# Two attention + GLU layers on one core: output normalization partly on GpSimd, layer norms in pairs, and a new order

## The chip, the cores and the metric

The kernel runs on one core of a Trainium2 chip. The time is device time in microseconds of one launch; several runs of a kernel are made and their median is given. The core's engines that matter here are TensorE (PE, with its weight loads PEld), VectorE (DVE), ScalarE (ACT), GpSimd (POOL) and SyncE (SP), whose queue carries nearly all DMAs.

## The reference

The input is x, 2048 rows (tokens) of 512 numbers in bf16. Two blocks are applied, and then the same two again with the same weights:

```python
def _layernorm(x, axis=-1, eps=1e-5):
    m = jnp.mean(x, axis=axis, keepdims=True)
    v = jnp.var(x, axis=axis, keepdims=True)
    return (x - m) / jnp.sqrt(v + eps)

def _A_ref(x, wqkv, wo):            # 32 heads of 16, window of 256 keys, causal
    q, k, v = split_heads(x @ wqkv)
    scores = einsum("bhqd,bhkd->bhqk", q, k) * (16 ** -0.5)
    scores = where(mask, scores, -1e9)      # 0 <= query - key < 256
    o = einsum("bhqk,bhkd->bhqd", softmax(scores), v)
    return merge_heads(o) @ wo

def _B_ref(x, w_gate, w_up, w_down):        # hidden width 1792
    return (sigmoid(x @ w_gate) * (x @ w_up)) @ w_down

x = x + _A_ref(_layernorm(x), A_wqkv, A_wo)
x = x + _B_ref(_layernorm(x), B_w_gate, B_w_up, B_w_down)
x = x + _A_ref(_layernorm(x), A_wqkv, A_wo)
x = x + _B_ref(_layernorm(x), B_w_gate, B_w_up, B_w_down)
```

`split_heads` and `merge_heads` stand here for the reference's reshapes and transposes.

## The kernel before

x stays in SBUF (`xsb`) as 16 tiles of 128 tokens. All the weights are loaded once.

For each tile and layer the work is this.

- **Layer norm** (`layer_norm`). VectorE computes the statistics (L600, L602). GpSimd adds the epsilon (L612) and raises to the power -1/2 (L613); this step is called `root`. VectorE applies them (L629) into a buffer `xn`. TensorE transposes the tile in four blocks (L647), and ScalarE or VectorE copies the result out of PSUM into `xnT` (L676 or L678, the lines of the copy helper). The normed tile feeds Q, K and V (key `"p"`) or the GLU (key `"g"`).
- **Q, K, V** (L713, L744, L780). The first two are computed for groups of four tiles, 512 columns at a time, apart from a few units of the first group that are cut by tile. K is split into even and odd heads by two multiplications on VectorE (L759).
- **Attention scores** in visits: a visit fills four PSUM banks (`Sps`) with scores (L1039, L1050, L1060), and ScalarE takes their exponential in one instruction (L1092) into `PTring` or `edge`. VectorE multiplies the borders of the window by masks (L970).
- **Values** (L1119): 80 small matmuls for half of the heads of a tile. The V matrix has a column of ones for each head, so the sum of the exponentials comes out beside the output. Two copies bring both halves into `OTs` (L676 or L678).
- **Normalization of the output** (`after_values`). VectorE turns the tile in 32 x 32 blocks (L1138, `OTs` to `Oq`), takes the reciprocals of the sums (L1144, `Rt`), multiplies in two instructions, one for even and one for odd heads (L1146, `On`), and turns the result back (L1151, `OnT`). Then TensorE applies the output projection (L903), VectorE adds it to x (L909), and the layer norm of the GLU begins.
- **GLU** (L808): gate and up projections, ScalarE's tanh (L826, the sigmoid in another form) and VectorE's product (L834) into `hT`, in groups of one, two or four tiles that `GLU` lists. Then the down projection (L872) and its sum with x (L881), followed by the next layer's norm or the output's DMA.

The order of all instructions is fixed when the program is built. The class `Plan` acts the engines' time out with a duration for each task, and whenever an engine falls free in it, the ready task with the lowest number in `PRIO` (later `LATE_PRIO`) goes next; TensorE's next work is chosen by `pick` and `choose`, with `RANK`. `PACE` holds the least time between visits in the plan: its entries 2 and 3 hold before the visit given by entry 4, after that entry 0 is for the first layer and entry 1 for the second. On the chip, each engine runs its instructions in the order that came out, and waits by semaphores. The duration and the priority stand in the call that makes a task:

```python
b = pl.task({"DVE": 1130}, turn, [box[0], box[1]], self.prio["oq0" if early else "oq"], lambda: self.has("Oq"), port=True)
c = pl.task({"DVE": 1030}, norm, [b.done], self.prio["no0" if early else "no"], lambda: self.has("On"), port=True)
d = pl.task({"DVE": 600}, turn2, [c.done], self.prio["on0" if early else "on"], lambda: self.has("OnT"), port=True)
```

`port=True` makes the plan keep such a task from running beside another task so marked on VectorE or GpSimd. Buffers come in rings (`ring`); there is one `OTs`, one `Oq`, one `Rt`, one `On` and two `OnT`.

Of the kernel before, what the change touches and what calls it, by code (L numbers as in the profile page):

```python
# [9 lines left out]
ALU = mybir.AluOpType  # L10
# [46 lines left out]
def pool_ns(n):  # L57
# [5 lines left out]
GLU = [[[1, 1, 1, 1, 2, 2], [1, 1, 1, 1, 2, 2], [1, 1, 2, 2, 2], [1, 1, 1, 1, 1, 1, 1, 1], [2, 2, 2, 2], [1, 1, 1, 1, 1, 1, 1, 1], [2, 2, 4]], [[4, 4, 4, 4], [4, 4, 4, 2, 1, 1], [4, 4, 2, 1, 1, 4]]]  # L63
PACE = [2681.81, 1328.37, 1196.7, 872.42, 21.95]
EARLY = 16
# [17 lines left out]
PRIO = dict(st_x0=8.026, ap_x0=7.059, xt_x0=10.785, st_x1=3.545, ap_x1=6.693, xt_x1=8.977, st_x=12.044,  # L83
    ap_x=12.327, xt_x=-6.634, st_p=-1.733, ap_p=4.349, xt_p=1.138, st_g=-6.356, ap_g=3.74, xt_g=-5.594,
    st_g0=3.292, ap_g0=-10.915, xt_g0=-4.847, tp=7.272, tp_g=6.212, q=-0.67, q0=11.129, q1=-22.989,
    k=-9.747, k0=14.768, k1=0.61, s=-5.3, s0=4.016, s1=2.634, v=0.444, v0=23.378, v1=20.074, vv=-6.331,
    exp=-13.785, exp0=-0.049, m0=3.46, m00=4.795, e0=-8.802, e00=0.423, e1=-0.562, e10=9.011, m2=-6.041,
    m20=0.716, th=15.676, mu=-10.778, dn=-20.12, add=2.096, add0=7.831, out=-15.994, mv=31.961, mv0=5.964,
    oq=-8.579, oq0=-11.733, no=13.392, no0=-3.279, on=11.451, on0=-10.714, vc=11.541, vc0=-1.273)
OPT = dict(gu='SP', g1=0, bk=3, bq=3, wide=0, r0=2, g0=5, g2=0, x0=1, eps=1, hold=1, own=1, ck=0, cq=2,  # L90
    turn=2, split=0, mo=0, at=3, r1=3, near=3)
SLACK = dict(xt=5595, oq=812, on=1665, vc=730)
RANK = dict(tp=-16.462, o=-6.977, lead=17.162, far=65.44, v=20.015, g=58.528, d=32.436, feed=40.797,
    x3=34839.477, wd=1492.629, go=176.096)
LATE_PRIO = dict(st_p=-4.956, ap_p=38.034, xt_p=0.962, st_x=-1.619, ap_x=-5.199, xt_x=17.448, st_g=-14.573,
    ap_g=-6.614, xt_g=0.299, q=-17.247, k=34.931, s=-1.549, v=-6.237, exp=-43.312, m0=4.641, e0=8.453,
    e1=11.689, m2=17.496, th=2.747, mu=-20.998, dn=2.523, add=-6.022, out=27.029, mv=45.566, oq=-5.883,
    no=8.561, on=11.817, vc=-20.116)
LATE_SLACK = dict(xt=541, oq=5451, on=4000, vc=10531)
LATE_RANK = dict(tp=52.672, o=-17.659, lead=2.057, far=12.106, v=-5.627, g=-3.049, d=10.813, feed=-60.763,  # L100
    go=344.346)
# [271 lines left out]
class Net:  # L373


    def __init__(self, ctx, tc, A_x, wqkv, wo, w_gate, w_up, w_down, out):
# [44 lines left out]
        ring("xn", 4, [P, 1, D])  # L421
# [164 lines left out]
    def layer_norm(self, key, t, deps):  # L586

        nc, pl = self.nc, self.pl
        done = self.xn_ready[key, t]
        box = {}  # L590
# [5 lines left out]
        def stats(e):  # L596
            if "st" not in box:
                box["st"] = self.take("st")
            st = box["st"][0][:, 0]
            nc.vector.bn_stats(out=st[:, 0:6], in_=self.xsb[:, t, :])  # L600
            if not first:
                nc.vector.bn_aggr(out=st[:, 6:8], in_=st[:, 0:6])  # L602

        def moments(e):
            st = box["st"][0][:, 0]
            nc.vector.bn_aggr(out=st[:, 6:8], in_=st[:, 0:6])
            nc.vector.tensor_scalar(out=st[:, 9:10], in0=st[:, 7:8], scalar1=1e-5, scalar2=None, op0=ALU.add)

        def root(e):
            st = box["st"][0]  # L610
            if not first:
                nc.gpsimd.tensor_scalar(out=st[:, 0, 9:10], in0=st[:, 0, 7:8], scalar1=1e-5, scalar2=None, op0=ALU.add)  # L612
            nc.gpsimd.tensor_tensor(out=st[:, 0, 8:9], in0=st[:, 0, 9:10], in1=self.nhalf[:, 0:1], op=ALU.pow)  # L613
# [10 lines left out]
        def apply(e):  # L624
            box["xn"] = b = self.take("xn")
            if key not in self.xnT:
                self.xnT[key] = self.take("xnT")
            st = box["st"][0][:, 0]
            nc.vector.tensor_scalar(out=b[0][:, 0, :], in0=self.xsb[:, t, :], scalar1=st[:, 6:7], scalar2=st[:, 8:9],  # L629
                                    op0=ALU.subtract, op1=ALU.mult)  # L630
# [6 lines left out]
        b = pl.task({"POOL": 800 - 230 * first}, root, [a.done], self.prio["st_" + kind])  # L637
        self.roots[key + (t,)] = b.done
        c = pl.task({"DVE": 406}, apply, [b.done], self.prio["ap_" + kind], can, port=True)
# [3 lines left out]
        i = t % NBG  # L643
        def steps(bank):
            pt = self.tp_view(bank)
            xn = box["xn"][0][:, 0]
            return [(57, lambda c=c: nc.tensor.transpose(pt[:, c, :], xn[:, c * P:(c + 1) * P], self.ident[:]))  # L647
                    for c in range(KT)]

        def evac(u):  # L650
            pt = self.tp_view(u.bank)
            if key == ("p", 0, 0) and t < OPT["split"]:
                half, both = KT // 2, Event()
                when_all([pl.task({e: ns}, lambda e, o=o: self.copy(e, self.xnT[key][0][:, i][:, o:o + half], pt[:, o:o + half]), [u.done],
                                  self.prio["tp"] - 9).done for e, ns, o in (("ACT", act_ns(half * P), 0), ("DVE", dve_ns(half * P) + 50, half))], both.fire)
                both.then(lambda: (self.give(box["xn"]), done.fire()))
                return both
            d = pl.task({"ACT": act_ns(KT * P), "DVE": dve_ns(KT * P) + 100}, lambda e: self.copy(
                e, self.xnT[key][0][:, i], pt), [u.done], self.prio["tp" if key[0] == "p" else "tp_g"])
            d.done.then(lambda: (self.give(box["xn"]), done.fire()))  # L660
            return d.done

        def ready():
            u = Unit(("tp", t), steps, [], False, evac)
            if key == ("p", 0, 0) and OPT["own"]:
                u.own = BANKS + t
            self.streams[0].append(u)

        c.done.then(ready)
# [455 lines left out]
    def after_values(self, L, t, half, bank, done):  # L1125
# [13 lines left out]

        def norm(e):  # L1140
            box["Rt"], box["On"] = self.take("Rt"), self.take("On")
            Oq, Rt, On = box["Oq"][0], box["Rt"][0], box["On"][0]
            tv = Oq[:].rearrange("p c (b r) -> p c b r", r=32)
            nc.vector.reciprocal(out=Rt[:], in_=tv[:, :, :, 16:17])  # L1144
            for e in range(2):
                nc.vector.tensor_tensor(out=On[:, :, :, e, :], in0=tv[:, e:8:2, :, 0:16],  # L1146
                                        in1=Rt[:, e:8:2].to_broadcast([P, 4, 4, 16]), op=ALU.mult)
# [10 lines left out]
        b = pl.task({"DVE": 1130}, turn, [box[0], box[1]], self.prio["oq0" if early else "oq"], lambda: self.has("Oq"), port=True)  # L1158
        b.done.then(lambda: self.give(box["OTs"]))
        c = pl.task({"DVE": 1030}, norm, [b.done], self.prio["no0" if early else "no"], lambda: self.has("On"), port=True)  # L1160
        c.done.then(lambda: (self.give(box["Oq"]), self.give(box["Rt"])))
        d = pl.task({"DVE": 600}, turn2, [c.done], self.prio["on0" if early else "on"], lambda: self.has("OnT"), port=True)
# [324 lines left out]
```

## Time and profile before

| | |
|---|---|
| median of 3 runs | 565.57 us (565.51 to 566.4) |
| the profiled execution | 566.81 us |
| its span, first to last instruction | 565.1 us |
| PE busy | 548.7 us (97%) |
| VectorE busy | 461.9 us (82%) |
| ScalarE busy | 407.8 us (72%) |
| GpSimd busy | 61.4 us (11%) |
| granted TensorE clock | 1.0 |

The profile gives every instruction's start and end with its line in the kernel. A row of a group reads: line, engine, operation, what it writes and reads, shape, count, then busy time in us and the mean ns of one, then the engine's idle time before these instructions and what ended most of it. A row of waits reads: engine, tile and line that waited, what it waited for, total us, times, and the longest. The first layer's attention runs to about 260 us, the second layer's from about 285 to 490 us in bursts; after about 496 us only GLU work of the second layer is left. DMA is busy mostly in the first 60 us.

### The profile page before, as it was taken

What the parts mean: (1) busy time and instruction counts of PE and PEld (TensorE: products, weight loads), DVE (VectorE), ACT (ScalarE), POOL (GpSimd) and SP (SyncE); (2) the same over time, 40 slices, a digit from 0 to 9 for tenths busy, and PEclk for the clock granted to TensorE, in tenths of its full rate; (3) what the DMA queues carried; (4) which work ended last, traced back from release to release, by engine and by line L of the source; (5) the groups of instructions that cost most, each with busy time, mean ns of one, the idle gap of its engine ahead of it and who ended that gap; (6) DMA issues with size and microseconds to landing.
All of it is one profiled execution on the core that took longest, in us unless ns stands there. A gap on an engine that the chain in (4) does not pass through costs nothing.

```text
span 565.1 us, 22076 instructions
## 1 busy us (share of the span) xinstructions
PE 548.7 (97%) x9998; PEld 300.0 (53%) x9998; DVE 461.9 (82%) x921; ACT 407.8 (72%) x424; POOL 61.4 (11%) x153
## 2 busy tenths in 40 slices
PE   8999899999999999999999999999999999999997
PEld 7446565854788645444444444544444444544443
DVE  6999999999988899996699986989768999852332
ACT  3999989979999887891699827999189985530330
POOL 4411111111101120101100011000100001000000
PEclk9999999999999999999999999999999999999999
DMA  8723000000000000000000000000100000000001
GB/s 254 294 92 106 3 24 2 23 3 23 4 23 3 23 3 23 23 2 1 11 2 23 3 13 11 2 23 3 40 20 2 23 3 31 12 1 20 19 0 38
DMA packets 18574, 17.38 MB, mean 31 GB/s; under 512 B 1841, under 2 KB 17457, under 8 KB 18481
## 3 DMA queue, kind: packets, MB, share of 16 engines
q1 hardware_dynamic: 17360, 14.93, 8.1%
q8 instruction: 78, 1.28, 0.9%
q10 hardware_dynamic: 1120, 1.05, 0.6%
q14 instruction: 16, 0.12, 0.1%
HBM read 9.70 MB, written 2.10 MB: 21 GB/s over the span
## 4 chain that ended last, share of the span: by engine, by line
PE 66%; DVE 21%; ACT 5%; issue 4%; DMA 2%; ACTq 1%; POOL 0%; SPq 0%; DVEq 0%
PE bank L808 29%; PE bank L872 14%; PE bank L1119 6%; PE Sps L1039 5%; PE bank L903 5%; DVE PTring L970 3%; DVE kTp L759 3%; PE bank L713 2%; DVE Oq L1138 2%; PE bank L780 2%; DVE edge L970 2%; ACT PTring L1092 2%; DVE On L1146 2%; DVE st L600 1%; DMA wg<-in_B_w_gate_dram 1%
## 5 line engine op out<-in xcount | busy, mean ns | idle before, releaser
L1092 ACT ACTIVATE PTring<-Sps 128x2048 bf16<-128x2048 f32 (+1 forms) x122 | 226.7, 1859 | 29.2 <-PE Sps L1039 26.6
L808 PE MATMUL bank<-xnT,wg 128*128 128x128 bf16 (+1 forms) x784 | 125.7, 288 | 1.3 <-ACT xnT L676 0.9
L808 PE MATMUL bank<-xnT,wu 128*128 128x128 bf16 (+1 forms) x784 | 125.6, 288 | 0.0
L872 PE MATMUL bank<-wd,hT 128*128 128x512 bf16 (+2 forms) x462 | 103.3, 373 | 0.0
L834 DVE SCALAR_TENSOR_TENSOR hT<-hT,bank 128x512 bf16<-128x512 bf16 (+1 forms) x140 | 78.0, 570 | 27.0 <-PE bank L808 23.1
L826 ACT ACTIVATE hT<-bank 128x512 bf16<-128x512 f32 (+1 forms) x140 | 69.3, 518 | 33.3 <-PE bank L808 33.1
L808 PEld LDWEIGHTS <-wg 128*128 128x128 bf16 x784 | 58.9, 98 | 40.4 <-issue 4.0
L808 PEld LDWEIGHTS <-wu 128*128 128x128 bf16 x784 | 59.1, 98 | 38.3 <-issue 2.3
L872 PEld LDWEIGHTS <-hT 128*128 128x128 bf16 x462 | 42.9, 98 | 49.2 <-issue 1.6
L612 POOL TENSOR_SCALAR st<-st 128x1 f32<-128x1 f32 x60 | 17.8, 297 | 426.1 <-DVE st L602 426.0
L1092 ACT ACTIVATE edge<-Sps 128x2048 bf16<-128x2048 f32 (+1 forms) x32 | 56.9, 1777 | 8.8 <-PE Sps L1050 8.1
L676 ACT COPY xnT<-bank 128x512 bf16<-128x512 bf16 x36 | 20.1, 603 | 46.4 <-PE bank L647 46.4
L1119 PE MATMUL bank<-PTring,Vaug 128*32 128x64 bf16 (+1 forms) x2880 | 52.5, 203 | 0.7 <-DVE PTring L970 0.5
L1039 PE MATMUL Sps<-qT,kTp 32*128 32x256 bf16 (+3 forms) x1216 | 47.5, 248 | 3.7 <-ACT PTring L1092 1.9
L1119 PEld LDWEIGHTS <-Vaug 128*32 128x32 bf16 x2880 | 44.1, 97 | 13.1 <-issue 11.1
L600 DVE BATCH_NORM_STATS2 st<-xsb 128x6 f32<-128x512 bf16 x64 | 43.7, 683 | 2.6 <-DMA xsb<-in_A_x_dram 2.2
L1119 PE MATMUL bank<-edge,Vl 128*32 128x64 bf16 x1024 | 44.2, 193 | 0.9 <-DVE edge L970 0.7
L881 DVE SCALAR_TENSOR_TENSOR xsb<-bank,xsb 128x512 bf16<-128x512 f32 (+2 forms) x33 | 22.0, 665 | 28.1 <-PE bank L872 28.0
L970 DVE TENSOR_TENSOR PTring<-PTring,mask 128x1024 bf16<-128x1024 bf16 x64 | 43.3, 678 | 1.2 <-ACT PTring L1092 1.0
L1039 PEld LDWEIGHTS <-kTp 32*128 32x128 bf16 x1216 | 18.8, 92 | 44.1 <-issue 41.1
L1138 DVE STREAM_TRANSPOSE Oq<-OTs 128x1024 bf16<-128x1024 bf16 x32 | 39.7, 1240 | 1.6 <-ACT OTs L676 1.0
L1119 PE MATMUL bank<-edge,Vh 128*32 128x64 bf16 x896 | 40.8, 193 | 0.0
(70 smaller groups left out, 691.0 us busy)
## 6 DMA issues: line engine op xcount, KB each, us to landing
Vl<-Vaug SPq DMA_DIRECT2D x32, 68.0 KB, 2.2
out_dram<-xsb SPq DMA_DIRECT2D x15, 128.0 KB, 2.1
Vh<-Vaug SPq DMA_DIRECT2D x28, 68.0 KB, 2.2
wg<-in_B_w_gate_dram SPq DMA_DIRECT2D x2, 896.0 KB, 9.2
wu<-in_B_w_up_dram SPq DMA_DIRECT2D x2, 896.0 KB, 11.8
wd<-in_B_w_down_dram SPq DMA_DIRECT2D x7, 256.0 KB, 3.7
xsb<-in_A_x_dram SPq DMA_DIRECT2D x6, 256.0 KB, 5.7
wq<-in_A_wqkv_dram SPq DMA_DIRECT2D x3, 256.0 KB, 5.7
```

The lines of the kernel that those rows point to most:

```text
L600: nc.vector.bn_stats(out=st[:, 0:6], in_=self.xsb[:, t, :])
L808: return [(mm_ns(w), lambda i=i, j=j, fc=fc, wt=wt, kt=kt: self.nc.tensor.matmul(pt[:, i, j, :], lhsT=wt[:, kt, fc * P:(fc + 1) * P], rhs= ...
L826: self.nc.scalar.activation(out=self.hT[:, ch[0] * GW:ch[0] * GW + size], in_=pt, func=AF.Tanh, scale=0.5)
L834: self.nc.vector.scalar_tensor_tensor(out=h, in0=h, scalar=1.0, in1=pt, op0=ALU.add, op1=ALU.mult)
L872: nc.tensor.matmul(self.banks[bank][:, 0:w], lhsT=self.hT[:, at:at + P], rhs=self.wd[:, fc, d], start=fc == 0, stop=fc == FC - 1)
L881: e = pl.task({"DVE": dve_ns(w)}, lambda e: nc.vector.scalar_tensor_tensor(out=self.xsb[:, t, d], in0=self.banks[u.bank][:, 0:w], scalar=0 ...
L903: return [(mm_ns(D), lambda c=c: nc.tensor.matmul(self.banks[bank][:], lhsT=b[0][:, c, :], rhs=self.wot[:, c, :], start=c == 0, stop=c == ...
L970: done = pl.task({"DVE": dve_bf_ns(1024)}, lambda e: nc.vector.tensor_tensor(out=r, in0=r, in1=m.to_broadcast([P, 16, HP]), op=ALU.mult), ...
L1039: nc.tensor.matmul(self.sps[:, m, o:o + n * HP], lhsT=kTp[32 * m:32 * m + 32, i, tt, e, :], rhs=self.qT[32 * m:32 * m + 32, i, q0:q0 + n * ...
L1092: nc.scalar.activation(out=out, in_=src, func=AF.Exp, scale=scale)
L1119: nc.tensor.matmul(o, lhsT=Va[:, c0:c0 + 32], rhs=p(h), start=k == 0 or t == 0, stop=k == len(parts) - 1 or t == 0, tile_position=(0, 32 * g))
L1138: nc.vector.transpose(out=box["Oq"][0][:].rearrange("p c q -> p (c q)"), in_=box["OTs"][0][:].rearrange("p c q -> p (c q)"))
```

## The change

In `after_values` the reciprocal becomes a task of its own on VectorE, and the two multiplications become a task on GpSimd, between the first and the second turn. This task has no `port` mark.

In `layer_norm` two neighbouring tiles share one task for the root, one task for applying (two instructions), one unit of eight transposes and one copy out of PSUM, which is 1024 wide. The first group of four tiles and the first two tiles of the first GLU stay alone, as all were. The `xn` ring has two buffers of two tiles in place of four of one.

The durations given to the plan change (1130 to 1260, 600 to 725, and others), and with them all its priorities, ranks and paces. The choice of the first layer's GLU groups changes: `g0` selects eight groups of one tile before, and 1, 1, 2, 2, 2 after, each followed by 4, 4. The second layer's (`g2`) are four of four in both. Of the first K and Q units, two and one are cut by tile, where it was three and three.

```diff
-GLU = [[[1, 1, 1, 1, 2, 2], [1, 1, 1, 1, 2, 2], [1, 1, 2, 2, 2], [1, 1, 1, 1, 1, 1, 1, 1], [2, 2, 2, 2], [1, 1, 1, 1, 1, 1, 1, 1], [2, 2, 4]], [[4, 4, 4, 4], [4, 4, 4, 2, 1, 1], [4, 4, 2, 1, 1, 4]]]
-PACE = [2681.81, 1328.37, 1196.7, 872.42, 21.95]
-EARLY = 16
+GLU = [[[1, 1, 2, 2, 2], [1, 1, 1, 1, 2, 2], [1, 1, 2, 2, 2], [1, 1, 1, 1, 2, 2], [2, 2, 2, 2], [1, 1, 1, 1, 1, 1, 1, 1], [2, 2, 4]], [[4, 4, 2, 1, 1, 1, 1, 2], [4, 2, 2, 4, 1, 1, 2], [4, 4, 4, 4]]]
+PACE = [1944.11, 1222.78, 405.97, 655.26, 5.98]
+EARLY = 12
...
-OPT = dict(gu='SP', g1=0, bk=3, bq=3, wide=0, r0=2, g0=5, g2=0, x0=1, eps=1, hold=1, own=1, ck=0, cq=2,
-    turn=2, split=0, mo=0, at=3, r1=3, near=3)
+OPT = dict(gu='SP', g1=0, bk=2, bq=1, wide=0, r0=2, g0=2, g2=2, x0=1, eps=1, hold=1, own=1, ck=0, cq=2,
+    turn=2, split=0, mo=0, at=3, r1=1, near=3)
...
-        ring("xn", 4, [P, 1, D])
+        ring("xn", 2, [P, 2, D])
...
+        alone = key[:2] == ("p", 0) and t < NBG * (1 + OPT["g1"]) or key[0] == "g" and key[1] * NT + t < 2
...
-        box = {}
+        if alone:
+            box, tiles = {"i": 0}, [t]
+        else:
+            box = self.pairs.setdefault((key, t // 2), {"i": t % 2, "ready": []})
+            tiles = [t // 2 * 2, t // 2 * 2 + 1]
...
+            for k, tt in enumerate(tiles):
+                st = box["st"][0][:, k]
+                nc.vector.tensor_scalar(out=b[0][:, k, :], in0=self.xsb[:, tt, :], scalar1=st[:, 6:7], scalar2=st[:, 8:9],
+                                        op0=ALU.subtract, op1=ALU.mult)
...
+        if not alone:
+            box["ready"].append(a.done)
+            if len(box["ready"]) < 2:
+                return
+        b = pl.task({"POOL": 800 - 230 * first}, root, box.get("ready", [a.done]), self.prio["st_" + kind])
...
+            def steps(bank):
+                pt = self.tp_view(bank, 2 * KT)
+                xn = box["xn"][0][:].rearrange("p t d -> p (t d)")
+                return [(57, lambda c=c: nc.tensor.transpose(pt[:, c, :], xn[:, c * P:(c + 1) * P], self.ident[:]))
+                        for c in range(2 * KT)]
+
+            def evac(u):
+                d = pl.task({"ACT": act_ns(2 * KT * P), "DVE": 670}, lambda e: self.copy(
+                    e, self.xnT[key][0][:, i:i + 2].rearrange("p t c q -> p (t c) q"), self.tp_view(u.bank, 2 * KT)),
+                    [u.done], self.prio["tp" if key[0] == "p" else "tp_g"])
...
+        def invert(e):
+            box["Rt"] = self.take("Rt")
+            nc.vector.reciprocal(out=box["Rt"][0][:], in_=box["Oq"][0][:].rearrange("p c (b r) -> p c b r", r=32)[:, :, :, 16:17])
+
         def norm(e):
-            box["Rt"], box["On"] = self.take("Rt"), self.take("On")
+            box["On"] = self.take("On")
...
-            nc.vector.reciprocal(out=Rt[:], in_=tv[:, :, :, 16:17])
             for e in range(2):
-                nc.vector.tensor_tensor(out=On[:, :, :, e, :], in0=tv[:, e:8:2, :, 0:16],
+                nc.gpsimd.tensor_tensor(out=On[:, :, :, e, :], in0=tv[:, e:8:2, :, 0:16],
                                         in1=Rt[:, e:8:2].to_broadcast([P, 4, 4, 16]), op=ALU.mult)
...
-        b = pl.task({"DVE": 1130}, turn, [box[0], box[1]], self.prio["oq0" if early else "oq"], lambda: self.has("Oq"), port=True)
+        b = pl.task({"DVE": 1260}, turn, [box[0], box[1]], self.prio["oq0" if early else "oq"], lambda: self.has("Oq"), port=True)
...
-        c = pl.task({"DVE": 1030}, norm, [b.done], self.prio["no0" if early else "no"], lambda: self.has("On"), port=True)
+        i = pl.task({"DVE": 370}, invert, [b.done], self.prio["no0" if early else "no"], lambda: self.has("Rt"), port=True)
+        c = pl.task({"POOL": 1300}, norm, [i.done], self.prio["no0" if early else "no"], lambda: self.has("On"))
...
-        d = pl.task({"DVE": 600}, turn2, [c.done], self.prio["on0" if early else "on"], lambda: self.has("OnT"), port=True)
+        d = pl.task({"DVE": 725}, turn2, [c.done], self.prio["on0" if early else "on"], lambda: self.has("OnT"), port=True)
```

`PRIO`, `SLACK`, `RANK`, `LATE_PRIO`, `LATE_SLACK` and `LATE_RANK` get new numbers throughout.

## The prediction

> **What bounds the kernel now.** I read the page's busy times first, then the same times in stretches of 20 us, then the waits, then single rows for prices.
>
> ```profile
> PE 548.7 (97%) x9998; PEld 300.0 (53%) x9998; DVE 461.9 (82%) x921; ACT 407.8 (72%) x424; POOL 61.4 (11%) x153
> ...
> PE 66%; DVE 21%; ACT 5%; issue 4%; DMA 2%; ACTq 1%; POOL 0%; SPq 0%; DVEq 0%
> ```
>
> TensorE is busy for 548.7 of 565.1 us, so its idle time is 16.4 us. VectorE holds a fifth of the chain that ended last, GpSimd none of it.
>
> ```profile
> 40.00:60.00 20.00, 17.93 (x448) 12.61 (x451) 19.76 (x44) 18.97 (x23) 4.26 (x10) 1.00 0.23 75
> ...
> 120.00:140.00 20.00, 20.00 (x397) 9.35 (x396) 19.59 (x40) 17.16 (x15) 3.06 (x6) 1.00 0.06 18
> 140.00:160.00 20.00, 19.20 (x559) 14.51 (x558) 17.04 (x36) 18.04 (x20) 2.10 (x4) 1.00 0.04 10
> ...
> 500.00:520.00 20.00, 20.00 (x95) 9.00 (x94) 6.92 (x11) 4.19 (x7) 0.00 (x0) 1.00 0.03 11
> ```
>
> In the stretches of 20 us the columns are PE, PEld, DVE, ACT, POOL. From 20 to 260 us (twelve rows, three of them above) DVE adds up to 226.2 of 240 us, or 94%, and PE to 233.0: first-layer attention runs on three full engines, and 7.0 us of PE's idle time lie there. From 280 to 500 us DVE is at 189.9 of 220 us and PE idles 2.1 us. After 500 us PE is alone. Less VectorE work can therefore pay mostly before 260 us.
>
> ```profile
> PE Sps L1039 <- ACT PTring L1092: 1.9, 4, 0.8
> ...
> PE bank L647 <- DVE Vaug L678: 1.2, 4, 0.6
> ...
> PE Sps L647 <- DVE xn L629: 1.1, 1, 1.1
> ...
> PE bank L808 <- ACT xnT L676: 0.9, 1, 0.9
> ...
> PE bank L1119 <- DVE edge L970: 0.7, 3, 0.4
> ```
>
> These are PE's own waits (total, times, longest). Those for VectorE (the three here, PTring 0.5, xnT 0.5, xn 0.3) make 4.3 us. A busy PE hides more: taking the ends of matmul records one after another and subtracting columns times 0.42 ns (the chain's 112 matmuls of 512 columns take 24.33 us) and about 0.12 to 0.16 us for each change between the three kinds of matmul (dense, scores, values), I count 29.7 us in 200 places above 60 ns each. About 11 us of it end on VectorE, 9 on ScalarE, the rest on nothing visible. So 4.3 to 11 us is all that a perfect VectorE could give back.
>
> **Prices** come from the groups of instructions by shape (busy time, then mean ns of one) and from three places of the timeline (start and length in us).
>
> ```profile
> L613 POOL TENSOR_TENSOR st<-st,nhalf 128x1 f32<-128x1 f32 x64 | 38.5, 602 | 11.1 <-DVE st L607 6.1
> ...
> L1146 DVE TENSOR_TENSOR On<-Oq,Rt 128x256 bf16<-128x256 bf16 x64 | 24.4, 422 | 1.1
> L676 ACT COPY xnT<-bank 128x512 bf16<-128x512 bf16 x36 | 20.1, 603 | 46.4 <-PE bank L647 46.4
> ...
> L678 DVE COPY xnT<-bank 128x512 bf16<-128x512 bf16 x24 | 9.3, 415 | 0.4 <-PE bank L647 0.3
> ...
> L1092 ACT ACTIVATE edge<-Sps 128x1024 bf16<-128x1024 f32 x4 | 4.1, 1033 | 2.0 <-PE Sps L1050 1.9
> ```
> ```profile
> 192.85 0.66 DVE L970 TENSOR_TENSOR PTring<-PTring,mask 128x1024 bf16<-128x1024 bf16 x1
> 193.03 0.57 POOL L612 TENSOR_SCALAR st<-st 128x1 f32<-128x1 f32 x1 [12.33 <-DVE st L602]
> ```
> ```profile
> 493.47 0.22 POOL L612 TENSOR_SCALAR st<-st 128x1 f32<-128x1 f32 x1 [13.91 <-DVE st L602]
> ```
> ```profile
> 12.79 0.68 DVE L759 TENSOR_SCALAR kTp<-kTp,rm 128x512 bf16<-128x512 bf16 x1 [0.35 <-ACT kTp L676]
> 12.80 0.47 POOL L543 MEMSET Vaug<- 128x64 bf16 x1
> ```
>
> **Multiplications to GpSimd.** VectorE loses 64 instructions, 24.4 us (0.76 a tile); 16 tiles, 12.2 us, belong to the full first layer. GpSimd gains 64. No row shows such an instruction there. Lower bound: VectorE's 0.42 us. Upper: 0.94, the longest L613. I take 0.65, half of the 1300 ns which the new code itself reckons for both, in the middle of the rows; that is 41.6 us in all. The pair's path grows by 1.3 - 0.76 = 0.5 us a tile, plus one more hop. Cover: from the end of the first turn (L1138) to the start of the second (L1151) the trace has 1.7 to 6.3 us, 3.8 on the mean of 32 tiles (117.3 to 122.0 for one), much of it other VectorE work, and PE has dense GLU work meanwhile. I cost it at 0; if the cover is gone it is 32 times 0.5, 16 us. Behind the multiplications on GpSimd's queue stand the roots (L612, L613) of a norm, which then wait up to 1.3 us, and apply (L629) behind them.
>
> **Who waits when both engines run.** A GpSimd instruction of 0.22 us took 0.57 when it met a mask multiplication (L970), and ended when that did; 12 of 60 L612 did so. The other way, L759 took 0.68 us instead of 0.35 beside GpSimd's memset. So some of the freed VectorE time comes back as masks that are held: nothing at least, and at most half of 0.65 us for each of 64, 20.8 us. I take half of that, 10.4: VectorE then gains 14 us net, 7 of it before 260 us. For PE: 0 to 10.4 us lost, since PE's order is fixed and its value matmuls wait for masks; I take 1.0, as the waits of L1119 for masks are only 1.2 us now.
> The Trainium skill, "SBUF — State Buffer", section "SBUF: two separate sides", speaks against the change: VectorE and GpSimd have one port pair, locked for a whole instruction, and the loser blocks fully. The rows above agree in kind. By the rule almost every multiplication would hold up a VectorE instruction, the gain of VectorE would shrink to 24.4 - 20.8 = 3.6 us, what PE gets back from 5 to about 1.3, and the sum to -0.2 us.
> The skill's "GPSIMD Engine Reference", section "3.1 Elementwise — side-by-side cycle accounting", has about 2.6 cycles of 1.2 GHz for an element of such an instruction, an estimate of 0.55 us for 256 without its start; no row here shows it, and by it the path would grow by 0.3 us a tile and the sum stay.
>
> **Norms by two.** Six tiles stay alone (four of the first group, GLU's first two), 58 become 29 pairs. Statistics and applications keep their number on VectorE. Roots fall from 60 + 64 to 31 + 35 instructions, 26 us less on GpSimd, off the path. Transposes keep their number. The copy out of PSUM doubles in width: ScalarE 1.03 us by the nearest row instead of 2 x 0.60, VectorE between 0.42 and 0.83. The engines save at most 0.2 to 0.4 us a pair, which I put at 0 for the end. But what waits for the copy waits 0.43 us longer: PE does at 525.2 us (0.94 us idle before the last group) and at 207.5. I take +1.0 for these two; all 29 pairs would be +12.5. The first tile of a pair also waits for its partner's attention, one tile later; PE has the previous tiles' GLU to do, and from tile 2 on first-layer GLU groups are now two wide, so they need both anyway. No DMA is added or moved past.
>
> **GLU groups.** First layer: from eight groups of one tile to 1,1,2,2,2, then 4,4 as now; second layer four of four as now. So 672 matmuls of 128 columns become 336 of 256. The chain's 17 of 128 columns take 0.95 us, 56 ns each; 256 columns lie between 109 (on the line to 217) and 112: 0 to -1.0 us, I take -0.8. The three K and Q units no longer cut by tile give -0.1. The chunks that ScalarE and VectorE take stay 256 wide.
>
> **The plan.** Every priority is new, so the order moves everywhere. What can be said from rows is that VectorE's turns were reckoned 1130 and 600 ns and last 1240 and 706, and the norm 1030 against 342 + 845: 0.37 us a tile that VectorE runs late where it is 94% full. The new figures are near the rows. With 7 us net freed before 260 us, and this, I give PE back 5 of the 11 us that end on VectorE.
>
> **Sum**: -0.8 - 0.1 - 5 (VectorE) + 1.0 (masks held) + 1.0 (wider copies) = -3.9 us. The profiled execution took 566.81 us (span 565.1 and 1.7 around it), 1.2 above the median; from it 562.9, and against the median of 565.57, which I forecast, **561.7 us**.
>
> **Rivals.**
> Held masks, slower: GpSimd's multiplication holds VectorE's masks, and PE, whose order is fixed, waits at L1119. Place: 20 to 260 us and the bursts after 288. Price 10.4, less the 0.9 of matmul work and a little relief: some +8.5, 574. It decides once a tile loses over about 0.2 us of PE to it (32 x 0.2 = 6.4, the gains above). For it: VectorE is 94% full, so nothing absorbs a hold. Against: L970 never exceeded 0.69 us in 180, even beside the short roots. Chance 0.28.
> Pairs starve the GLU, slower: half of the 29 pairs delay PE by 0.43, +6, less 3 of relief: 568.5. For it: the 0.94 at 525 us. Against: PE's full rows elsewhere. Chance 0.15.
> The plan takes all that VectorE holds, faster: -11 - 0.9, 553.7. For it: VectorE at 94%; against: ScalarE is at 17 to 19 of 20 us in the same rows and would be the next late. Chance 0.12.
> Nothing moves: GpSimd's holds give back what VectorE gained, 565.3. Chance 0.08.
> Forecast: 0.37, from 558 to 564.
>
> **How the numbers follow.** About 0.2% (1.1 us) is what a measurement of this kernel can tell from no change. Faster 0.37 + 0.12 = 0.49; same 0.08; slower 0.28 + 0.15 = 0.43. Both signs hold much, so the forecast's own range, 558 to 564, stands beside the whole one: 554 to 574 leaves out a little over half of each outer rival's far side.
>
> **What would show it.** Right: L1146 on GpSimd near 1.3 us for two, DVE's row between 437 and 448 us, PE's idle time under 13 us with 20 to 60 us gaining most, L970 with few rows over 0.7 us. Held masks: L970 rows of 0.9 us and more, and PE waiting for PTring or edge for several us. Pairs: waits of L808 and L780 for xnT. Wrong altogether: a longer stretch after 490 us with PE alone and VectorE idle, or PE with dense work lacking in the first layer because attention ran ahead.

## The result and the profile after

The changed kernel takes 567.42 us (median of 10 runs, 567.18 to 567.52) against 566.0 for the kernel before in the same comparison: a ratio of 1.0024 with a 95% interval of 1.0014 to 1.0033. It is 1.4 us slower. The forecast was 561.7 (558 to 564), 3.9 us faster. The profiled execution took 567.18 us with a span of 565.2. The one before took 566.81 with a span of 565.1, longer than any of the ten timed runs of its kernel; so the two traces show the difference only in part.

The page's busy times and engines of the chain:

```profile
PE 540.2 (96%) x9566; PEld 291.5 (52%) x9626; DVE 459.7 (81%) x862; ACT 396.5 (70%) x390; POOL 95.2 (17%) x159
...
PE 64%; DVE 26%; ACT 4%; issue 3%; POOL 2%; DMA 0%; DVEq 0%; ACTq 0%; POOLq 0%
```

VectorE lost 24.4 us of multiplications and is busy for only 2.2 us less (461.9 to 459.7). Its share of the chain rose from 21 to 26%. PE's busy time can't be compared: 60 matmul records are missing after (9566 beside 9626 weight loads), none before.

Groups by shape, with busy time and mean ns. First the masks before:

```profile
L970 DVE TENSOR_TENSOR edge<-edge,maske 128x1024 bf16<-128x1024 bf16 x60 | 40.3, 683 | 0.0
...
L970 DVE TENSOR_TENSOR PTring<-PTring,maskn 128x1024 bf16<-128x1024 bf16 x56 | 37.6, 672 | 1.1 <-ACT PTring L1092 0.9
```

Then after (L1178 is the multiplication, L999 the masks and L707 VectorE's copies, in the new numbering):

```profile
L1178 POOL TENSOR_TENSOR On<-Oq,Rt 128x256 bf16<-128x256 bf16 x64 | 54.9, 878 | 256.1 <-DVE Rt L1171 256.1
...
L999 DVE TENSOR_TENSOR edge<-edge,maske 128x1024 bf16<-128x1024 bf16 x60 | 46.7, 793 | 0.0
...
L999 DVE TENSOR_TENSOR PTring<-PTring,maskn 128x1024 bf16<-128x1024 bf16 x56 | 39.7, 712 | 0.0
...
L707 DVE COPY xnT<-bank 128x1024 bf16<-128x1024 bf16 x20 | 13.5, 677 | 0.0
```

GpSimd's multiplication lasts 878 ns on the mean, 2.1 times VectorE's 422. That mean has two parts: 18 of the 64 take 0.61 to 0.64 us, and each of the other 46 (0.66 to 1.16 us) ends 0.46 to 0.50 us after a VectorE instruction that was running beside it, a mask in 44 of them. So each engine makes the other longer; an instruction that takes longer because of the other engine's is called held here. The edge masks went from 683 to 793 ns and the maskn ones from 672 to 712; over the three kinds of mask, count times mean, VectorE spends 131.1 us instead of 122.0. Copies out of PSUM take another part: VectorE's CAST and COPY add up to 71.7 us after and 61.8 before, ScalarE's to 62.8 and 80.5. About 1.0 us of VectorE's 9.9 is one copy of a mask at the start, the rest is work that the new order gives to VectorE. About half of it, 4.8 us, is the normed x: VectorE copied 24 of the 64 tiles before, and now copies 43 (20 pairs, as in the last row above, and 3 single tiles). So 9.1 us went to longer masks and some 9 to copies out of PSUM.

One tile in the timeline, GpSimd, VectorE and PE:

```profile
145.28 1.00 POOL L620 TENSOR_TENSOR st<-st,nhalf 128x2 f32<-128x2 f32 x1
146.25 1.64 POOL L1178 TENSOR_TENSOR On<-Oq,Rt 128x256 bf16<-128x256 bf16 x2
```
```profile
146.30 1.12 DVE L999 TENSOR_TENSOR PTring<-PTring,maskn 128x1024 bf16<-128x1024 bf16 x1
147.92 0.71 DVE L1183 STREAM_TRANSPOSE OnT<-On 128x512 bf16<-128x512 bf16 x1 [0.51 <-POOL On L1178]
148.56 0.65 DVE L999 TENSOR_TENSOR PTring<-PTring,mask 128x1024 bf16<-128x1024 bf16 x1
```
```profile
148.92 0.81 PE L932 MATMUL bank<-wot,OnT 128*128 128x512 bf16 x3 [1.37 <-DVE OnT L1183]
```

A mask starts 0.05 us after GpSimd's two multiplications have begun and takes 1.12 us instead of 0.67. Then VectorE stands for 0.51 us before the second turn, and a mask that is behind the turn in its queue stands too. PE, whose next instruction is the output projection, idles 1.37 us. Of the 180 masks 26 take over 0.74 us, 10.8 us beyond 0.68 in all; none did before.

PE's own waits for the normed x:

```profile
PE bank L809 <- DVE xnT L707: 2.5, 4, 0.7
...
PE bank L837 <- DVE xnT L707: 0.9, 1, 0.9
...
PE bank L742 <- DVE xnT L707: 0.7, 2, 0.5
```

With 0.7 us on ScalarE's copies these are 4.8 us, where it was 1.4. Its waits for `OnT` and, at the value matmuls (L1148), for masks:

```profile
PE bank L932 <- DVE OnT L1183: 1.6, 2, 1.4
...
PE bank L1148 <- DVE edge L999: 0.9, 3, 0.5
```

For `OnT` PE waited 0.3 us before. With 0.2 us for `PTring` the waits for masks are 1.1 us, where they were 1.2: the masks are held, but it isn't at the value matmuls that PE waits for them.

### The profile page after: what moved, and what is told of

Its sections match the earlier page's. It is cut to its first block, busy times and chain, and to the rows that moved or that the text cites. A ratio compares the mean times of both kernels' runs of the same rounds, so it can differ in the third digit from the quotient of the medians.

```text
span 565.2 us, 21171 instructions
## 1 busy us (share of the span) xinstructions
PE 540.2 (96%) x9566; PEld 291.5 (52%) x9626; DVE 459.7 (81%) x862; ACT 396.5 (70%) x390; POOL 95.2 (17%) x159
## 4 chain that ended last, share of the span: by engine, by line
PE 64%; DVE 26%; ACT 4%; issue 3%; POOL 2%; DMA 0%; DVEq 0%; ACTq 0%; POOLq 0%
PE bank L837 29%; PE bank L901 13%; PE bank L1148 6%; PE Sps L1068 5%; PE bank L932 4%; DVE PTring L999 4%; DVE kTp L788 3%; PE bank L742 3%; DVE st L606 2%; DVE Oq L1167 2%; DVE edge L999 2%; ACT PTring L1121 2%; PE bank L809 2%; DVE xn L638 2%; DVE xnT L707 2%
## 5 line engine op out<-in xcount | busy, mean ns | idle before, releaser
L837 PE MATMUL bank<-xnT,wg 128*128 128x512 bf16 (+2 forms) x616 | 126.4, 322 | 2.1 <-DVE xnT L707 0.9
L837 PE MATMUL bank<-xnT,wu 128*128 128x512 bf16 (+2 forms) x616 | 125.4, 321 | 0.2 <-issue 0.2
L901 PE MATMUL bank<-wd,hT 128*128 128x512 bf16 (+2 forms) x444 | 100.3, 373 | 1.7 <-issue 1.3
L1178 POOL TENSOR_TENSOR On<-Oq,Rt 128x256 bf16<-128x256 bf16 x64 | 54.9, 878 | 256.1 <-DVE Rt L1171 256.1
L837 PEld LDWEIGHTS <-wu 128*128 128x128 bf16 x616 | 55.1, 98 | 42.1 <-issue 3.0
L837 PEld LDWEIGHTS <-wg 128*128 128x128 bf16 x616 | 53.5, 98 | 42.6 <-issue 6.0
L1148 PE MATMUL bank<-PTring,Vaug 128*32 128x64 bf16 (+1 forms) x2880 | 52.1, 203 | 0.2 <-DVE PTring L999 0.2
L1148 PEld LDWEIGHTS <-Vaug 128*32 128x32 bf16 x2880 | 43.9, 97 | 13.4 <-issue 11.9
L999 DVE TENSOR_TENSOR edge<-edge,maske 128x1024 bf16<-128x1024 bf16 x60 | 46.7, 793 | 0.0
L1148 PE MATMUL bank<-edge,Vl 128*32 128x64 bf16 x1024 | 44.2, 193 | 1.0 <-DVE edge L999 0.9
L999 DVE TENSOR_TENSOR PTring<-PTring,mask 128x1024 bf16<-128x1024 bf16 x64 | 43.6, 682 | 0.9 <-ACT PTring L1121 0.7
L707 DVE CAST OTs<-bank 128x512 bf16<-128x512 f32 x42 | 30.6, 728 | 12.6 <-PE bank L1148 12.6
## 6 DMA issues: line engine op xcount, KB each, us to landing
wu<-in_B_w_up_dram SPq DMA_DIRECT2D x2, 896.0 KB, 12.4
```

The source lines that it names most:

```text
L707: self.nc.vector.tensor_copy(out=out, in_=in_)
L837: return [(mm_ns(w), lambda i=i, j=j, fc=fc, wt=wt, kt=kt: self.nc.tensor.matmul(pt[:, i, j, :], lhsT=wt[:, kt, fc * P:(fc + 1) * P], rhs= ...
L901: nc.tensor.matmul(self.banks[bank][:, 0:w], lhsT=self.hT[:, at:at + P], rhs=self.wd[:, fc, d], start=fc == 0, stop=fc == FC - 1)
L999: done = pl.task({"DVE": dve_bf_ns(1024)}, lambda e: nc.vector.tensor_tensor(out=r, in0=r, in1=m.to_broadcast([P, 16, HP]), op=ALU.mult), ...
L1148: nc.tensor.matmul(o, lhsT=Va[:, c0:c0 + 32], rhs=p(h), start=k == 0 or t == 0, stop=k == len(parts) - 1 or t == 0, tile_position=(0, 32 * g))
L1178: nc.gpsimd.tensor_tensor(out=On[:, :, :, e, :], in0=tv[:, e:8:2, :, 0:16], in1=Rt[:, e:8:2].to_broadcast([P, 4, 4, 16]), op=ALU.mult)
```

## The experiments

Theories: H, GpSimd's multiplications hold VectorE back and lengthen the way to `OnT`, and PE, in its fixed order, waits; N, VectorE's time reaches PE little either way; R, the relief is worth several us and something else of the change lost them. The first runs keep the order of all other instructions: the plan is left as it was, and only what a task issues is edited. Where a ratio is given it is to the kernel before on the same chip; 0.1% is 0.57 us. VectorE's busy time is given from each run's page, to set beside 461.9 us before and 459.7 after.

**e1, the kernel before with the multiplications on GpSimd.**
```diff
-nc.vector.tensor_tensor(out=On[:, :, :, e, :], ...
+nc.gpsimd.tensor_tensor(out=On[:, :, :, e, :], ...
```


> The kernel before with its order of instructions kept, only the two multiplications of the output's normalization issued on GpSimd at the place where VectorE had them; the plan still reckons them as VectorE's. Theory H (GpSimd holds VectorE's masks and lengthens the path to OnT, and PE waits for it): slower than before by 3 to 8 us, masks (L970) with rows up to 1.1 us and PE waiting for OnT. Theory N (VectorE's time is not what limits, neither relief nor holds reach PE): within 1.5 us of before.

566.71 us, ratio 1.0016 (1.0007 to 1.0025): 0.9 us slower. The masks on edges went to 774 ns on the mean, and the second turn now waits:

```profile
DVE OnT L1151 <- POOL On L1146: 8.9, 11, 1.3
PEld L903 <- DVE OnT L1151: 6.8, 11, 1.5
PE bank L903 <- DVE OnT L1151: 2.9, 7, 1.0
```

H's signs are there, but its size is not, and N's size alone would fit. VectorE is busy for 446.3 us, 15.6 less than before, and yet the end is later. The next runs show why: two large terms cancel.

**e2, the changed kernel with the multiplications on VectorE.**
```diff
-nc.gpsimd.tensor_tensor(out=On[:, :, :, e, :], ...
+nc.vector.tensor_tensor(out=On[:, :, :, e, :], ...
```


> The changed kernel with its order kept, only the two multiplications issued on VectorE again, at the place in the order where GpSimd's began. Theory H: faster than the changed kernel by 1 to 4 us, as nothing is held any more and two multiplications take 0.8 instead of 1.7 us. Theory N: within 1 us of it. Theory R (the relief of VectorE was worth several us and something else of the change lost them): slower by 2 to 5 us.

569.12 us, ratio 1.0059 (1.0047 to 1.0072), against the changed kernel's 1.0024: 2 us slower than it. That is theory R's figure; H's was the wrong way. In this order GpSimd is the better place, by little. VectorE's row:

```profile
L1178 DVE TENSOR_TENSOR On<-Oq,Rt 128x256 bf16<-128x256 bf16 x64 | 23.9, 416 | 0.1
```

It is also 3.4 us slower than the kernel before, with the multiplications on the same engine as there: with them on VectorE, pairs, GLU groups and the new order together cost 3.4 us. VectorE is busy for 468.4 us, 6.5 more than before. The order was made for multiplications on GpSimd, so another one might do better with them on VectorE.

**e3 and e4, the multiplications nearly taken away**, on GpSimd after, on VectorE before.
```diff
-out=On[:, :, :, e, :],   in0=tv[:, e:8:2, :, 0:16], in1=Rt[:, e:8:2].to_broadcast([P, 4, 4, 16])
+out=On[:, :, :, e, 0:1], in0=tv[:, e:8:2, :, 0:1],  in1=Rt[:, e:8:2].to_broadcast([P, 4, 4, 1])
```


> The changed kernel with its order kept; GpSimd multiplies only one of each 16 columns (the rest of On stays zero), so that its instructions are short and hold VectorE little. Theory H: faster than the changed kernel by 4 to 8 us, and the masks back at 0.68 us. Theory N: faster by at most 1 us. Theory R gives at most 2 us.

561.47 us, ratio 0.9922 (0.9910 to 0.9934). From the changed kernel's 1.0024 that is 1.0% or 5.8 us: H's range. VectorE is busy for 449.4 us. Masks are back at 668 to 676 ns, those on edges for one:

```profile
L1000 DVE TENSOR_TENSOR edge<-edge,maske 128x1024 bf16<-128x1024 bf16 x60 | 39.5, 673 | 0.0
```

> The kernel before with its order kept; VectorE multiplies only one of each 16 columns (the rest of On stays zero), which frees it of most of the 24 us without GpSimd. It measures what relief alone is worth in a given order. The recorded prediction put 5 us on the relief: by it and by theory R faster by 3 to 6 us; theory N: at most 1 us; theory H says nothing of this one, as nothing is held.

562.16 us, ratio 0.9937 (0.9924 to 0.9951): 3.6 us faster, with 64 instructions of 225 instead of 422 ns, 12.6 us less. Relief is worth 0.29 us for each us of VectorE in this order. N falls. The changed kernel with equally short multiplications on VectorE (e13 below) is 0.7 us faster by the ratios; so pairs, GLU groups and the new order give 0.7 us here, where in e2 they cost 3.4. What they are worth depends on how much VectorE has to do.

**e5, holds without the path.** After short multiplications, two of full size into a tile that nobody reads.
```diff
+            for e in range(2):
+                nc.gpsimd.tensor_tensor(out=self.spare[:], in0=tv[:, e:8:2, :, 0:16],
+                                        in1=Rt[:, e:8:2].to_broadcast([P, 4, 4, 16]), op=ALU.mult)
```


> The changed kernel's order; the multiplications that OnT waits for are the short ones (one of 16 columns, the rest of On stays zero), and after them GpSimd runs two of full size into a spare tile that nobody reads. So the path is as short as in the kernel with short multiplications alone (561.5 us), but VectorE's masks can be held as in the changed kernel (567.4). If holding is what costs: 565 to 568 us. If the longer way to OnT costs: 561 to 563 us. Roots of norms can also stand longer behind GpSimd's extra work.

563.74 us, ratio 0.9958 (0.9946 to 0.9970), 2.0 us over e3: between the two expectations. But the masks took only 4.0 us more than in e3 where the changed kernel's take 10.1 more; the extra instructions came 1 us later, and 16 masks took over 0.74 us instead of 26.

**e6 and e9, the path without holds.** A power of 128 x 2 numbers ahead of the short multiplications. The line is that of e9, where it reads `Rt`; in e6 it reads two other columns of `spare`.
```diff
+            nc.gpsimd.tensor_tensor(out=self.spare[:, 0:2], in0=Rt[:, 0:2, 0, 0], in1=self.nhalf[:, 0:2], op=ALU.pow)
```


> The changed kernel's order; in place of the full multiplications GpSimd runs one power of 128 x 2 numbers (about 0.7 us, which held no mask in the kernel before) and then the two short multiplications (one of 16 columns, the rest of On stays zero), so OnT's path is about the 1.7 us of the changed kernel while little can be held. If the longer way to OnT costs: 565 to 568 us. If holding costs: 561.5 to 563 us.

561.70 us, ratio 0.9922 (0.9910 to 0.9935), as e3. This run missed its aim: the power needed nothing from VectorE and ran ahead of the reciprocal, so the time from the reciprocal's end to the end of `On` stayed at 1.14 us (e3: 1.13).

> As the run with a power ahead of the short multiplications, but the power now reads Rt, so that GpSimd can't start it before the reciprocal is there and the way from the reciprocal to On is really about 1.7 us. On's other columns stay zero. The changed kernel's order; next to nothing is held. If the longer way to OnT costs by itself: 564.5 to 567 us. If only holds cost: 561.5 to 562.5 us. If the two work together (a held mask delays, and the second turn that waits for GpSimd stops all that stands behind it on VectorE): 562.5 to 564.5 us.

562.2 us, ratio 0.9929 (0.9916 to 0.9942). The way was 1.68 us now (the changed kernel: 1.91), no mask took over 0.74 us, and it cost 0.4 us by the ratios, 0.7 by the medians. The second turn waits for GpSimd for 4.3 us in all, where it is 4.5 in the changed kernel, and GpSimd is taken for about as long in each tile (0.92 + 2 x 0.35 = 1.6 us against 1.7), so roots of norms behind it are no dearer in the changed kernel either: `xn` waits for them for 1.8 us in both. The longer path by itself costs next to nothing in this order, whose plan had reckoned 1300 ns on GpSimd.

**e13 and e14, holds at the place where the changed kernel has them.** Short multiplications on VectorE; e14 adds the full ones on GpSimd, for nobody.
```diff
 e13: nc.vector.tensor_tensor(out=On[:, :, :, e, 0:1], ...
 e14: the same, then the spare multiplications of e5
```


> The changed kernel's order; short multiplications (one of 16 columns, the rest of On stays zero) on VectorE, none on GpSimd. Nothing is held and the path is shortest, but VectorE has 0.3 us a tile more than with the short ones on GpSimd (561.5 us). It is the base for the next run: 562 to 565 us.

561.77 us, ratio 0.9924 (0.9912 to 0.9936): faster than expected, as good as e3, though VectorE is busy for 4.7 us more than there (454.1 us). Against e2 it has 14.3 us less and is 7.6 us faster by the ratios, 0.53 us for each us. So the first 0.3 us a tile cost nothing, and what comes on top costs half of its time. e5 has the same busy time as e13 (453.8 us) and is 1.9 us slower: there, held masks cost what as much work elsewhere did not.

> As the run before it (short multiplications on VectorE, the rest of On zero), with two multiplications of full size on GpSimd into a spare tile that nobody reads, issued at the place where the changed kernel has them. OnT does not wait for them. If holds at this place are what the changed kernel pays: 4 to 7 us slower than the run before it, with about 10 us of masks held. If the second turn's wait for GpSimd is needed for it: 1 to 3 us slower.

569.82 us, ratio 1.0062 (1.0048 to 1.0076): 8.1 us slower than e13 on the same chip, above the 4 to 7 that holds alone should have cost, though nothing waits for what was added. Groups of e14 by shape:

```profile
L1183 POOL TENSOR_TENSOR spare<-Oq,Rt 128x256 bf16<-128x256 bf16 x64 | 56.2, 879 | 257.5 <-DVE Rt L1173 255.0
...
L1001 DVE TENSOR_TENSOR edge<-edge,maske 128x1024 bf16<-128x1024 bf16 x60 | 43.1, 726 | 0.0
...
L1180 DVE TENSOR_TENSOR On<-Oq,Rt 128x16 bf16<-128x16 bf16 x64 | 19.8, 376 | 0.1
```

and the last of these in e13:

```profile
L1179 DVE TENSOR_TENSOR On<-Oq,Rt 128x16 bf16<-128x16 bf16 x64 | 9.7, 219 | 0.1
```

Masks take 3.7 us more than in e13, less than the 10 expected, but the short multiplications themselves went from 219 to 376 ns on the mean, 10.0 us more: in most tiles the first of the two, which began after GpSimd's, took about 0.64 us, and the second 0.22. VectorE is busy for 468.0 us, 13.9 more than in e13, for 8.1 of the end: 0.58 us for each us. So this run doesn't repeat the changed kernel's holds; it shows what holds cost without a path through GpSimd. In the changed kernel VectorE's masks, K splits and norms are 11.7 us longer than in e3 (10.1 + 1.0 + 0.6) and its busy time 10.3 us, for 5.8 us: 0.56. As the path alone cost 0.4 to 0.7 (e9), holds account for most of the 5.8.

**e7, e15 and e16, half on each engine.** The edit of e7; in e15 the line taken out has `nc.gpsimd`, and e16 cuts GpSimd's half in two.
```diff
-nc.vector.tensor_tensor(out=On[:, :, :, e, :], ...
+(nc.vector, nc.gpsimd)[e].tensor_tensor(out=On[:, :, :, e, :], ...
```


> The kernel before with its order kept; only the multiplication of the odd heads is issued on GpSimd, the one of the even heads stays on VectorE, so that they run beside each other. If the costs add up in proportion: halfway between before (565.7) and all on GpSimd (566.7), 566.2. If slack swallows short delays (0.9 us of GpSimd instead of 1.7 in the path, VectorE still 12 us lighter): 564 to 565.5, faster than both kernels.

565.31 us, ratio 0.9985 (0.9976 to 0.9993), 0.85 us faster than before: the one complete kernel here that beats both. The second turn waits 0.5 us for GpSimd in all (e1: 8.9), and VectorE's own multiplication keeps its 425 ns; it begins 45 to 110 ns ahead of GpSimd's in all 32 tiles, and GpSimd's is the longer one:

```profile
L1146 POOL TENSOR_TENSOR On<-Oq,Rt 128x256 bf16<-128x256 bf16 x32 | 27.4, 857 | 154.8 <-DVE Rt L1144 154.8
...
L1146 DVE TENSOR_TENSOR On<-Oq,Rt 128x256 bf16<-128x256 bf16 x32 | 13.6, 425 | 1.1
```

> The changed kernel's order; the even heads' multiplication on VectorE, the odd heads' on GpSimd, beside each other. Between all on GpSimd (567.4) and all on VectorE (569.1) if costs add up: 568. If they are convex, as in the kernel before (565.3 for half against 566.0 and 566.7): 565 to 567 us.

569.76 us, ratio 1.0063 (1.0051 to 1.0076): slower than all on either engine. Here VectorE's half began 0.1 to 0.5 us after GpSimd's in 22 of 32 tiles, and there took 0.76 to 0.84 us:

```profile
L1178 DVE TENSOR_TENSOR On<-Oq,Rt 128x256 bf16<-128x256 bf16 x32 | 22.7, 711 | 0.1
```

711 against 416 ns (e2) gives back 9.4 of the 13.3 us that VectorE was spared. Costs are neither proportional nor convex; they go by what meets what, and which of the two began first. The old order shows something else too: from e7 to e1 masks take no more time (128.4 and 127.2 us), VectorE is busy for 12.4 us less, and yet the end is 1.8 us later, while the second turn's waits for GpSimd go from 0.5 to 8.9 us. In an order that was not planned for it, the longer path seems to cost.

> The kernel before in its order with the odd heads' multiplication on GpSimd (565.3 us), that one now in two instructions of half the size. If what a mask loses is the rest of one GpSimd instruction: held time well below the 6.7 us of the run with one instruction, and 564 to 565.2 us. If more instructions mean more starts and a longer path: 565.3 to 566.5 us.

565.71 us, ratio 0.9989 (0.9977 to 1.0001). Masks lost 3.7 us instead of 6.7, as expected of shorter instructions, but the time can't be told from e7's.

**e8, e10, e11 and e12, planned again.**
```diff
 e8:  -c = pl.task({"POOL": 1300}, norm, ...)       +c = pl.task({"POOL": 1760}, norm, ..., port=True)
 e10: the changed layer_norm in the kernel before, ring("xn", 2, [P, 2, D])
 e11: 1130 -> 1260, 1030 -> 1190, 600 -> 725
 e12: -PACE = [2681.81, ...]                        +PACE = [2670.0, ...]
```


> The changed kernel planned again with all its priorities, but GpSimd's multiplications reckoned at 1760 ns, as the trace shows, instead of 1300, and marked as using the port, so that the plan keeps VectorE's marked tasks from running beside them. If the plan's ignorance of the hold and of the duration is what loses: faster than the changed kernel, 564 to 566.5. If priorities found for one set of durations are worth little with another: slower, 568 to 574.

569.49 us, ratio 1.0069 (1.0051 to 1.0087), 2.5 us slower than the changed kernel. Masks were held less (edges 731 ns on the mean), but PE's waits of L837 for xnT, one of its waits, went from 0.9 to 4.7 us.

> Control for the runs that are planned again: the kernel before with one number of the plan changed by 0.4% (the pace of the first layer's visits, 2681.81 to 2670), which reorders instructions and changes no work. If an order is as good as another made from nearly the same numbers: within 1 us of before. If its priorities fit one order only: 1 to 6 us slower.

583.92 us, ratio 1.0314 (1.0298 to 1.0330): 17.8 us for 0.4% of one number, three times what I had allowed. It does no other work; PE's waits and part of its clock are worse. Stretches of its trace (PE, PEld, DVE, ACT, POOL, then the granted clock):

```profile
325.00:330.00 5.00, 3.03 (x106) 1.81 (x106) 4.92 (x12) 4.92 (x5) 0.00 (x0) 1.00 0.01 3
330.00:335.00 5.00, 3.91 (x17) 1.53 (x18) 3.75 (x10) 3.17 (x3) 2.36 (x6) 0.52 0.00 0
```

> The kernel before with the changed kernel's layer norm in pairs alone (xn ring, shared root, transposes and copy, copy durations as before), planned again with the priorities of before; output multiplications stay on VectorE, GLU groups of one tile as before. If pairs cost little, as predicted (1 us): as the control with a slightly changed pace. If PE's longer waits for xnT cost: 4 to 10 us slower than that control.

579.33 us, ratio 1.0234 (1.0219 to 1.0250): 4.6 us faster than the control, where even "little" had meant equal to it.

> The kernel before planned again with VectorE's turns and multiplications at 1260, 1190 and 725 ns instead of 1130, 1030 and 600, close to what its trace shows. If durations nearer to the rows make a better order by themselves: 562 to 565 us. If priorities found for the old figures count for more: as the control, 566 to 572.

593.44 us, ratio 1.0468 (1.0423 to 1.0512), outside both expectations, at a mean clock of 0.97. The control says that a neighbouring order of this kernel, planned with priorities found for another, can differ by 18 us without any cause in the work. So neither what pairs nor what durations cost at the end can be judged from e10 and e11. One thing of e10's trace does not depend on the end: VectorE's copies add up to 71.4 us, as in the changed kernel (71.7), and to 61.4 in its control e12. It is with the pairs that the plan gives VectorE more of the copies.

## Why the prediction was wrong

**What bounds the kernel** held: PE is nearly full, and VectorE's time reaches the end only in part. No run passes "4.3 to 11 us is all that a perfect VectorE could give back" (4.9 rather than 4.3, as two rows of 0.3 us for hT and OnT were left out): e4 gave 3.6 us, and e3 is 7.7 us faster than e2 by the ratios, in another order. No run frees VectorE altogether.

**The step that failed is the one from VectorE's time to the end**: "-5 (VectorE)" and "+1.0 (masks held)", -4.0 us together. What VectorE gains was sized in the right region: 14 us net was taken, and its busy time falls by 8.7 us in the new order (e2 to the changed kernel) and by 15.6 in the old one (before to e1). But the end moved by -2.0 us in the new order and by +0.9 in the old one, not by -4.0. The relief was there: -7.7 (e2 to e3), -3.6 for half of it in the old order (e4). What took most of it back, or more than all, is GpSimd's multiplication at full length: +5.8 in the new order (e3 to the changed kernel), most of it by holds, and +4.5 in the old one (e4 to e1), where no run parts holds from the path. The sum had taken the 10.4 us of holds off the relief (at its own 5 us for 14 that is 3.7), and then "I take 1.0, as the waits of L1119 for masks are only 1.2 us now". Those waits were the wrong row: they are 1.1 us after, and what grew are PE's waits for OnT (0.3 to 1.6 us) and for xnT (1.4 to 4.8). A held mask delays all that stands behind it in VectorE's order, not value matmuls alone. Nor has VectorE's time one rate, as the sum assumed: 0.29 us for each us in e4, nothing for the first 4.7 us from e3 to e13, 0.5 to 0.6 beyond.

**A second step was short too: pairs, groups and the new order.** The sum has +0.1 for them (-0.8, -0.1, +1.0), and "The engines save at most 0.2 to 0.4 us a pair, which I put at 0". With the multiplications on VectorE they cost 3.4 us (e2 against before); with short ones they give 0.7 (e13 against e4). VectorE saved nothing by the wider copies; it took over some 9 us of copies, and is busy for 6.5 us more in e2 than before. An estimate from the rates of e4 and e13, 0.29 to 0.53 us for each us, makes that 1.9 to 3.4 us of the end; no run isolates it.

How the 5.3 us between -3.9 and +1.4 split depends on the way that is taken: over e2 it is 3.3 for pairs, groups and order and 2.0 for the move to GpSimd; over e1 it is 4.9 for the move and 0.4 for the rest.

**The multiplication** was sized 0.65 us. That is near the 0.62 us that it takes where nothing holds it; with the holds it took 0.88 on the mean, within the range of 0.42 to 0.94. Its longer path, costed at 0, cost 0.4 to 0.7 in the new order (e9): right there.

**Roots**: GpSimd is busy for 21.2 us less with pairs (e2, 40.2 against 61.4), not 26, and off the path as expected.

**Wider copies**, +1.0: PE's own waits for xnT rose by 3.4 us in the trace. No run isolates what the end lost by it. **Matmul work**, -0.8: the ends of 256-column matmuls follow at 109 ns (median), two of 128 at 112, which is the far end of its range, -1.0; no run shows it at the end.

**The plan**: "I give PE back 5 of the 11 us that end on VectorE", partly for the truer durations. Nothing shows that truer durations give a better order; e11 was 27 us slower, but after the 18 us of e12 that says nothing against them either.

**The rivals.** Held masks, given 0.28, had the mechanism and one of its signs, masks over 0.9 us. The other sign failed: PE did not wait for masks at L1119. Its 574 was too high because it set "a little relief" beside the full hold. Nothing moves, given 0.08, had the right balance, "GpSimd's holds give back what VectorE gained", at -0.3 us against the measured +1.4. For the new order that balance leaves out the copies.

The Trainium skill's rule ("SBUF — State Buffer", section "SBUF: two separate sides": one port pair, locked for an instruction, the loser blocks) told the direction better than the rows that I chose: by it the prediction had a sum of -0.2 us. The holds agree with it in kind, 11.7 us against the 20.8 that the prediction has for nearly every multiplication holding something. What is left to be found is what meets: in e7 VectorE's half kept its 425 ns, in e15 it took 711.

What stays open: what pairs and the moved copies cost by themselves, how much of e1's 4.5 us is path, why e8 lost 2.5 us, and whether an order searched anew with holds in its plan would win.

## What to carry to other kernels

Work moved from VectorE to GpSimd isn't gone from VectorE: look in the trace for VectorE's two-input instructions that will run beside it, and price the time they lose by what stands behind them in VectorE's order, not by the waits that PE has now. In the trace after, look at which engine took over other work: here the copies went to VectorE. To learn what an engine's time is worth, shorten its instructions in the same order (e4, 0.29 us for each us) before planning anything, and don't carry the rate to another order (e13, 0.53). Where an order is searched, run a control that changes one number slightly; here it cost 18 us, so the time of a replanned kernel alone tells little of the edit that it was planned for.

## What was unexpected of the hardware

A GpSimd multiplication slowed even a VectorE instruction of 16 columns, from 219 to 376 ns on the mean of 64 (e14; about 0.64 us for the first of a tile's two). And GpSimd's own went from 0.62 us to as much as 1.16 beside VectorE's masks. After 5 us in which PE was busy for only 3.03, the granted clock was 0.52 for the next 5 us (e12, 325 to 335 us), in the middle of a kernel whose clock had been 1.00 for 320 us; the profiled executions that kept their order have 1.00 on the mean.
